# Attention and a gated product: issue order by fixed step gaps against issue order by a list scheduler

## The chip, the cores and the metric

The kernel runs on one core of one Trainium2 chip. Five engines work in it, each with its own queue of instructions that it takes strictly in order: TensorE (PE), VectorE (DVE), ScalarE (ACT), GpSimd (POOL), and SyncE (SP), which here only issues transfers between the chip's large memory and the on-chip one (SBUF). They meet through semaphores: an instruction waits until what it needs is there, and everything behind it on its queue waits with it. Matrix products leave PE into PSUM, a memory of eight banks, and DVE or ACT read them from there; POOL cannot.

The metric is the device time of one execution in microseconds. Less is better.

## The reference

```python
k_p = k.reshape(B, H, Sp, pool, D).mean(axis=3)       # B, H, S, D = 8, 8, 576, 64; pool = 8; Sp = 72
v_p = v.reshape(B, H, Sp, pool, D).mean(axis=3)
scores = scale * np.matmul(q, k_p.transpose(0, 1, 3, 2))
scores = scores - np.max(scores, axis=-1, keepdims=True)
attn = np.exp(scores)
attn = attn / (np.sum(attn, axis=-1, keepdims=True) + 1e-09)
attn_out = np.matmul(attn, v_p)

x = attn_out.transpose(0, 2, 1, 3).reshape(B * S, H * D)          # 4608 x 512
a, b = x @ w_a, x @ w_b                                # w_a, w_b: 512 x 1536
out = a * b @ w_out                                    # w_out: 1536 x 512
```

Keys and values are averaged over groups of eight positions, so each query attends to 72 keys. The result feeds a gated product: two inner products, their elementwise product, and an outer product. All is float32 outside. Inside, each number is kept as a high part, rounded for TensorE, and a low part (the number minus its high part), and a product is made of three matmuls: high by high, high by low, low by high. That is why so many instructions are casts and subtractions.

## The kernel before

**Tiling.** The 4608 rows (tokens) are cut into twelve halves of 384, and two halves make a pair. The first pair is computed in the plain way (`normal`), half by half; for the five others (`block`) a scheme with seven products in place of eight is used (Strassen's, in the form of Winograd): the right operands are sums and differences of parts of x (`prepare` makes them, T1 to T4), the left ones are sums and differences of parts of the weights (`block_sums` makes them, S1 to S4). Features are taken in steps of 256, so there are six items (steps) per pair and 30 seven-product items in all. The first pair has eight items: two of half 0, four of both halves, two of half 1. After each item, `outer` multiplies the gated features by w_out and DVE or ACT adds the result to the rows `y` (`taken_outer`), which go out after the pair's last item.

**Three streams.** Attention runs in 40 chunks of up to 128 queries (`chunk`): cast the queries, scores on PE, maximum, difference, exponential, sum, division, cast and split of the weights, transposes on PE, product with the values on PE. Keys and values of each of the eight batches are averaged by `load_keys` and `load_values`. Only three chunks belong to half 0, and the first weight product needs them. Meanwhile the weights, which arrive as 64-bit words, are converted (`convert_weights`: two ACT scalings and two DVE joins for each of 12 features and three matrices), split (`split_inner`, `split_outer`) and stored to memory (`keep`), since SBUF cannot hold them all. From then on every pass streams them back in (`load_parts`).

**What sets the order.** The program is written out by generators under the class `Chains` (lines 81 to 115). Its time is not in microseconds: it is a count of steps, and one step is about one group of matmuls on PE. A chain says "go on after so many steps", and the gaps are constants at the head (`PROBS_GAP`, `VALUE_GAP`, `CHUNK`, `KEYS_AHEAD`, `STORE_AFTER`, `BLOCK_STEPS` and so on). Which engine does a subtraction is written in the code. PE's main loop (lines 1038 to 1060) goes through the items in order, and between two groups of the present item it puts one group of `outer` of the item before:

```python
for _ in (normal if item[0] == "n" else block)(item):
    if next(before, "over") != "over":
        step()
```

**Tiles.** `Ring` gives out tiles in fixed rings: three of 4 KB per partition for raw weights, four and four for inner weight parts (`we`, `ws`), four for outer ones (`wo`): 15 in all, and each use has its own. The loads of the inner parts go round two or three rings in a fixed turn. In PSUM, attention has two banks (`att`), the inner products have four (`XA`, `XB`, `YA`, `YB`), the outer ones two (`acc`); the three chunks of half 0 also use the four (`early_bank`). The block sums are made, stored, and in every round, the first too, loaded from memory (`wanted`). Weight words are loaded by ACT's DMA queue, everything else by SP's.

## Time and profile before

| | |
|---|---|
| median of 3 runs | 1124.23 us (1123.45 to 1126.3) |
| profiled execution, its own time | 1121.22 us |
| profiled execution, span from first to last instruction | 1119.4 us |
| mean granted clock of PE | 0.966 |
| PE busy | 1013.6 us (91%), 5424 matmuls |
| DVE, ACT, POOL busy | 638.4, 466.7, 503.0 us |
| moved by DMA | 251.6 MB, 225 GB/s in the mean |

Shares of busy time are means over stages with different limits, so the prediction reads them by stretch. A busy PE is not a PE at its peak, since matmuls overlap and a lower granted clock makes each of them longer. In the list of groups a line is a line of the kernel; all subtractions for low parts have line 209, so there one goes by the names of the tiles. A row "A <- B" under waits says what A was waiting for last.

### The profile page before, as it was taken

The page shows a single profiled execution, that of the slowest core. Times are in us where ns is not written, and L with a number is a line of the kernel's source. Part 1 is how long each engine was busy: PE and PEld are TensorE (multiplying, and loading weights), DVE is VectorE, ACT ScalarE, POOL GpSimd, SP SyncE. Part 2 cuts the span into 40 slices and gives each one's busy share as a digit, 9 for nine tenths or more (in the row PEclk, how much of TensorE's full clock was granted, in tenths as well). Part 3 has the DMA queues.
Part 4 walks back from the last instruction along what each step waited for, and adds up shares of the span by engine and source line. Part 5 has one row for each costly group of instructions (what it writes and reads, how often), then busy time and mean ns, then how long its engine had stood idle before and what let it go on. Part 6 is the DMA issues. An engine that isn't in the chain of part 4 may idle for free.

```text
span 1119.4 us, 15231 instructions
## 1 busy us (share of the span) xinstructions
PE 1013.6 (91%) x5424; PEld 931.8 (83%) x5424; DVE 638.4 (57%) x1067; ACT 466.7 (42%) x1006; POOL 503.0 (45%) x462
## 2 busy tenths in 40 slices
PE   3368787998999979799999998999899999999998
PEld 3267687897889969789899897999799999999997
DVE  7697775746644653755754774463974453523333
ACT  3675656543445434334433444333434433322221
POOL 5344433374557855733333453433444442523322
PEclk9977799999989989899999999999999999999999
DMA  6687776458977985767644576456566455575441
GB/s 206 241 287 283 260 258 223 144 208 299 303 265 251 323 294 198 291 245 266 219 161 177 214 275 220 178 175 234 202 224 236 174 186 203 212 253 205 177 165 56
DMA packets 82586, 251.60 MB, mean 225 GB/s; under 512 B 12976, under 2 KB 12976, under 8 KB 82512
## 3 DMA queue, kind: packets, MB, share of 16 engines
q1 hardware_dynamic: 77328, 231.77, 58.5%
q10 hardware_dynamic: 5184, 18.88, 4.9%
q8 instruction: 43, 0.70, 0.2%
q14 instruction: 31, 0.25, 0.1%
HBM read 203.42 MB, written 47.19 MB: 224 GB/s over the span
## 4 chain that ended last, share of the span: by engine, by line
PE 59%; DVE 15%; DMA 13%; ACT 5%; POOL 3%; issue 3%; SPq 1%; ACTq 0%; POOLq 0%; DVEq 0%
PE acc_s L950 6%; PE acc_s L952 6%; PE acc_s L951 6%; DMA kept_S<-we 4%; PE psXA L868 3%; PE psXB L868 3%; PE psXA L870 3%; PE psXA L869 3%; PE psXB L869 3%; PE psXB L870 3%; DMA vraw<-in_vr 3%; DMA vraw<-in_v 2%; PE psYA L868 2%; PE psYB L868 2%; PE psYA L869 2%
## 5 line engine op out<-in xcount | busy, mean ns | idle before, releaser
L209 POOL TENSOR_TENSOR hh<-h,hh 128x384 fp32r<-128x384 f32 x144 | 150.6, 1052 | 128.6 <-ACT hh L905 80.8
L899 POOL TENSOR_TENSOR h<-h,h 128x384 f32<-128x384 f32 x90 | 98.1, 1090 | 231.5 <-DVE h L894 213.6
L975 DVE TENSOR_TENSOR y<-acc_s,y 128x512 f32<-128x512 f32 x150 | 102.9, 687 | 134.8 <-PE acc_s L952 134.5
L950 PE MATMUL acc_s<-wo,hh 128*128 128x512 f32 x360 | 144.8, 402 | 2.6 <-ACT y L973 2.6
L951 PE MATMUL acc_s<-wo,hh 128*128 128x512 f32 x360 | 142.8, 397 | 0.0
L952 PE MATMUL acc_s<-wo,hh 128*128 128x512 f32 x360 | 142.7, 396 | 0.0
L563 POOL TENSOR_TENSOR s<-s,z 128x576 f32<-128x576 f32 (+1 forms) x39 | 49.6, 1272 | 111.6 <-DVE z L561 102.3
L888 ACT COPY h<-psXA 128x384 f32<-128x384 f32 x90 | 43.1, 479 | 125.2 <-PE psXA L870 125.1
L952 PEld LDWEIGHTS acc_s<-wo,hh 128*128 128x128 f32 x360 | 68.2, 189 | 15.9
L950 PEld LDWEIGHTS acc_s<-wo,hh 128*128 128x128 f32 x360 | 68.3, 190 | 11.4 <-ACT y L973 2.9
L951 PEld LDWEIGHTS acc_s<-wo,hh 128*128 128x128 f32 x360 | 68.3, 190 | 8.3
L894 DVE TENSOR_TENSOR h<-psYA,h 128x384 f32<-128x384 f32 x60 | 33.2, 554 | 65.8 <-PE psYA L870 58.7
L905 ACT CAST hh<-h 128x384 fp32r<-128x384 f32 x90 | 45.5, 515 | 58.6 <-POOL h L899 58.2
L557 ACT ACTIVATE s<-s 128x576 f32<-128x576 f32 (+1 forms) x40 | 27.4, 685 | 100.9 <-DVE s L509 100.9
L598 PEld LDWEIGHTS ptr<-ident,pr 128*128 128x128 f32 (+1 forms) x320 | 36.1, 146 | 38.0 <-ACT pr L572 15.3
L599 ACT CAST turned<-ptr 128x512 fp32r<-128x512 f32 (+1 forms) x80 | 43.2, 544 | 55.8 <-PE ptr L598 53.7
L209 POOL TENSOR_TENSOR pr<-s,pr 128x512 fp32r<-128x512 f32 (+1 forms) x40 | 52.9, 1323 | 25.2 <-ACT pr L572 19.5
L598 PE MATMUL ptr<-ident,pr 128*128 128x128 f32 (+1 forms) x320 | 40.6, 253 | 25.8 <-ACT pr L572 12.2
L544 DVE TENSOR_REDUCE s<-psc 128x144 f32<-128x288 f32 (+1 forms) x104 | 42.7, 449 | 36.3 <-PE psc L541 36.2
L432 DVE TENSOR_REDUCE vp<-vraw 128x64 f32<-128x512 f32 (+1 forms) x42 | 27.4, 678 | 34.1 <-DMA vraw<-in_v 22.3
L209 DVE TENSOR_TENSOR ql<-tmp,qh 128x512 fp32r<-128x512 f32 (+1 forms) x37 | 34.5, 932 | 19.3 <-ACT qh L490 19.3
L572 ACT CAST pr<-s 128x512 fp32r<-128x512 f32 (+1 forms) x40 | 24.8, 621 | 49.1 <-POOL s L563 49.1
(359 smaller groups left out, 3053.2 us busy)
## 6 DMA issues: line engine op xcount, KB each, us to landing
wo<-kept_o SPq DMA_DIRECT2D x64, 512.0 KB, 4.7
we<-kept_S SPq DMA_DIRECT2D x44, 512.0 KB, 5.6
ws<-kept_S SPq DMA_DIRECT2D x44, 512.0 KB, 6.2
ws<-kept SPq DMA_DIRECT2D x41, 512.0 KB, 6.1
we<-kept SPq DMA_DIRECT2D x33, 512.0 KB, 4.7
raw<-kept_S SPq DMA_DIRECT2D x32, 512.0 KB, 3.8
kept<-we SPq DMA_DIRECT2D x24, 512.0 KB, 5.8
kept_S<-we SPq DMA_DIRECT2D x24, 512.0 KB, 6.0
```

What stands on the lines that cost most here:

```text
L209: eng.tensor_tensor(out=lo, in0=src, in1=hi.bitcast(F32), op=ALU.subtract)
L563: (nc.vector if first and i % 2 else nc.gpsimd).tensor_tensor(out=s[:n], in0=s[:n], in1=z[:n].unsqueeze(2).broadcast_to([n, H, SP]), op=AL ...
L598: nc.tensor.transpose(ptr[:rows, g, :n], src, ident[:n, :n])
L868: nc.tensor.matmul(pt, e[:, 0, m, c], xo[:, 0, kk], start=(opens and kk == 0), stop=False, **more)
L869: nc.tensor.matmul(pt, e[:, 0, m, c], xo[:, 1, kk], start=False, stop=False, **more)
L870: nc.tensor.matmul(pt, e[:, 1, m, c], xo[:, 0, kk], start=False, stop=(kk == 1), **more)
L899: nc.gpsimd.tensor_tensor(out=t, in0=t, in1=a, op=ALU.mult)
L905: nc.scalar.copy(e[:, 0], t)
L950: nc.tensor.matmul(pt, e[:, 0, cs], wos[y][:, 0], start=(y == 0), stop=False)
L951: nc.tensor.matmul(pt, e[:, 0, cs], wos[y][:, 1], start=False, stop=False)
L952: nc.tensor.matmul(pt, e[:, 1, cs], wos[y][:, 0], start=False, stop=(y == 1))
L975: nc.vector.tensor_tensor(out=acc[row], in0=pt, in1=acc[row], op=ALU.add)
```

## The change

`Chains` and `Ring` go. In their place stands `Machine`, a model of the five engines in microseconds, run while the program is built. Each piece of work asks for an engine (`on_pe`, `on_act`, `on_dve`, `either`, `transfer`) with a price and a rank; whenever the model's engine is free, it takes the waiting piece of the lowest rank and issues its instructions, and the piece goes on when the model says that it has ended, plus 0.25 us (`SETTLE`). So the order on each queue is the order in which the model's engine took the work.

- Ranks: attention chunks and weight features by a due time in microseconds, computed from fixed lengths of the items (27.0 for a block, 13.0 for a half); releases of tiles and readings of PSUM first (`TOP`), loads of parts 1e3, `outer` and stores 1e4, inner products 2e4. So PE takes attention first, then an outer group as soon as its operands are ready, and an inner group otherwise.
- `either`: subtractions, the gate's product and the division of the weights go to DVE or POOL, whichever the model has free first. Before, the engine was fixed.
- All transfers go through SP, the weight words too; the model lets SP run at most 3 us ahead of the landings, at 300 KB/us.
- `Slots`: one set of 15 tiles of 4 KB for early inputs, raw weights, words, inner and outer parts, raw reloads, sums and T2, each kind with a quota. Four smaller tiles (`tmp`) have quotas of their own.
- PSUM: until the first weight product all six banks besides `acc` serve attention; then it keeps two.
- Block sums of the first round are used straight from the tile in which they were made (they are stored as well); four inner parts that nobody reads again are no longer stored.
- The weights of attention lie in two fixed tiles with a 73rd column of 1e-9, so that the sum includes it; for batches 1 to 7 the keys are scaled over all four head pairs at once.

The number of matmuls is the same.

```diff
-class Chains:
-    def step(self, groups=1):
-        due = []
-        while self.chains and self.chains[0][0] <= self.now:
-            due.append(heapq.heappop(self.chains))
...
+    def take(self, engine):
+        queue = self.queues[engine]
+        while queue and queue[0][-1]["taken"]:
+            heapq.heappop(queue)
+        if not queue or self.free[engine] > self.now:
+            return False
+        asked = heapq.heappop(queue)[-1]
+        asked["taken"] = True
+        time = asked["time"][engine]
+        asked["issue"](engine)
+        end = self.free[engine] = self.now + time
+        self.later(end, None)
+        if engine == "SP":
+            self.landing = max(self.landing, end + 1.2) + asked["bytes"] / 300e3
+            self.free[engine] = max(end, self.landing - BACKLOG)
+            self.later(self.free[engine], None)
+            self.later(self.landing + 1.0, asked["job"])
+        else:
+            self.later(end if engine == "PE" else end + self.SETTLE, asked["job"])
+        return True
...
+def dve(n, ops=1):
+    return 0.1 * ops + 0.0012 * n
+def act(n, ops=1):
+    return 0.07 * ops + 0.00093 * n
+def pool(n, ops=1):
+    return 0.2 * ops + 0.00225 * n
+def mms(count, n):
+    return count * max(0.113, 0.013 + 0.00043 * n)
...
+QUOTA = {"early": 10, "raw": 3, "words": 3, "own": 4, "wo": 4, "load": 7, "raw2": 3, "sum": 4, "T2": 1}
+NSLOT = 15
...
+    def either(n, issue, ops=1):
+        return {"time": {"DVE": dve(n, ops), "POOL": pool(n, ops)}, "issue": lambda e: issue(engines[e])}
...
-        low_part(nc.gpsimd if first else nc.vector, ql[:, :, :n], qraw[:, :, :n], qh[:, :, :n])
+        yield low(NK * n, ql[:, :, :n], qraw[:, :, :n], qh[:, :, :n])
...
-            nc.scalar.dma_start(areas[f % 2], w_dram[name][:, f, :].bitcast(I32))
+            yield transfer(areas[f % 2], w_dram[name][:, f, :].bitcast(I32), 1 << 19)
...
-        nc.vector.tensor_reduce(out=z[:n], in_=s[:n], axis=AX.X, op=ALU.add)
-        nc.vector.tensor_scalar_add(z[:n], z[:n], 1e-9)
-        nc.vector.reciprocal(z[:n], z[:n])
+            nc.vector.tensor_reduce(out=z[:n], in_=wide[:n], axis=AX.X, op=ALU.add)
+            nc.vector.reciprocal(z[:n], z[:n])
...
+            if x in second and name[1] in ("S1", "S2", "S3", "S4"):
+                yield lambda: name in sums
+                loaded[x] = "sum", name, sums[name]
+                continue
+            yield lambda: name in kept and slots.can("load")() and x - taken["i"] < 9
...
+    psum = {"free": ["att0", "att1", "XA", "XB", "YA", "YB"], "att": {"att0", "att1"}, "opening": True}
...
+                    yield on_pe(mms(6, DM), products, 1e4)
+                yield on_pe(mms(6, HB), products, 2e4)
...
-        before = iter(())
-        for x, item in enumerate(items):
...
+        start(1e4, outer())
+        start(2e4, inner())
+        m.run()
```

More of the change, by code (lines that the diff above doesn't have):

```diff
@@ L87, in mark @@
+NSLOT = 15
+class Machine:
+    SETTLE = 0.25
+    def __init__(self):
+        self.now, self.count = 0.0, 0
+        self.queues = {e: [] for e in ("PE", "DVE", "ACT", "POOL", "SP")}
+        self.free = dict.fromkeys(self.queues, 0.0)
+        self.events, self.waiting, self.done = [], [], set()
+        self.landing = 0.0
     def mark(self, *what):
         self.done.add(what)
-    def wait(self, *marks):
-        while not all(m in self.done for m in marks if not isinstance(m[-1], int) or m[-1] >= 0):
-            yield 1
@@ L94, in start, with until @@
-    def start(self, chain, rank, after=0):
+    def until(self, *marks):
+        marks = [m for m in marks if not isinstance(m[-1], int) or m[-1] >= 0]
+        return lambda: all(m in self.done for m in marks)
+    def start(self, rank, task):
         self.count += 1
-        heapq.heappush(self.chains, (self.now + after, rank, self.count, chain))
-    def resume(self, chain, rank):
-        later = next(chain, None)
-        if later == self.PE:
-            self.count += 1
-            heapq.heappush(self.wanting, (rank, self.count, chain))
-        elif later is not None:
-            self.start(chain, rank, later)
@@ L325, in block_sums, with split_outer @@
+    def split_outer(f):
+        yield until(("weight", "o", f))
+        yield lambda: slots.can("wo")() and order_o[next_o[0]] == ("own", f)
+        next_o[0] += 1
+        e = slots.take("wo", ("own", f), [P, 2, 512], F32R)
+        w = rawt.pop(("o", f))
+        yield on_act(512, lambda: nc.scalar.copy(e[:, 0], w))
+        yield low(512, e[:, 1], w, e[:, 0])
+        tmps.give("o", f)
+        parts["o", f] = e
+        start(1e4 + f, keep("wo", ("o", f), e, False))
     def block_sums(j):
@@ L354, in block_sums, with load_raw @@
+            e = slots.take("sum", (j, name), e_shape, F32R)
+            yield on_act(512, lambda: nc.scalar.copy(e[:, 0], t))
+            yield low(512, e[:, 1], t, e[:, 0])
+            sums[j, name] = e
+            start(1e4, keep("sum", (j, name), e, False))
         for f in (2 * j, 2 * j + 1):
-            raws.give(("raw2", f))
+            slots.give("raw2", f)
         mark("sums", j)
+    def load_raw(f, t):
+        yield transfer(t.rearrange("p m c -> p (m c)"), kept["raw", f], 1 << 19)
+        mark("raw2", f)
@@ L620, in chunk @@
             if p > 1:
-                yield from wait(("prepared", p - 1))
+                yield until(("prepared", p - 1))
+            else:
+                yield lambda: all(("raw", f) in kept for f in range(3))
             if p not in xraw:
@@ new lines, in load_outer, with inner @@
+    def load_outer():
+        for x, name in enumerate(order_o):
+            if name[0] == "own":
+                continue
+            yield lambda: at_item[0] >= NJ - 1 and name in kept and slots.can("wo")() and next_o[0] == x
+            next_o[0] += 1
+            e = slots.take("wo", x, [P, 2, 512], F32R)
+            start(1e3 + x, load_one(x, ("wo", x, e), e.bitcast(F32).rearrange("p l c -> p (l c)"), kept[name], loaded_o))
+    def inner():
+        for number, item in enumerate(items):
+            at_item[0] = number
+            if item[0] == "n":
+                yield from normal(item)
+            else:
+                yield from block(item)
@@ new lines, in give_slot, with finish @@
+    def give_slot(e):
+        yield m.SETTLE
+        slots.give(e[0], e[1])
+    first_gate = {}
+    gated_in = [0]
+    def finish(item, f, half, h, key):
+        number = items.index(item)
+        need = sum(2 * len(x[1]) if x[0] == "n" else 4 for x in items[:number])
+        yield lambda: gated.can("hh")() and gated_in[0] >= need
+        gated_in[0] += 1
+        e = gated.take("hh", (item, f, half), [P, 2, HB], F32R)
+        yield on_act(HB, lambda: nc.scalar.copy(e[:, 0], h))
+        yield low(HB, e[:, 1], h, e[:, 0])
+        gates.give("h", key)
+        gs[item, f, half] = e
```

1333 lines of the change are left out of this document (680 added, 653 removed).

## The prediction

> **What bounds the kernel now.** I read the page's head and its slices first, then busy time by stretch, then what TensorE (PE) waited for, then the opening on VectorE (DVE), the groups of instructions and the DMA issues.
>
> ```profile
> span 1119.4 us, 15231 instructions
> PE 1013.6 (91%) x5424; PEld 931.8 (83%) x5424; DVE 638.4 (57%) x1067; ACT 466.7 (42%) x1006; POOL 503.0 (45%) x462
> PEclk9977799999989989899999999999999999999999
> ```
>
> PE is the bound of the whole, but not of every stage. The next view has, for each stretch: its length, then busy time and count of PE, PE's weight loads, DVE, ACT and POOL, then the granted clock, the DMA share and GB/s. The cuts are the first product with the weights (62.6), the first seven-product block (292.9), and places where the idle time changes.
>
> ```profile
> 0.00:62.60 62.60, 24.78 (x110) 20.97 (x111) 46.25 (x79) 30.25 (x64) 29.46 (x37) 0.99 0.65 216
> 62.60:292.90 230.30, 197.74 (x1049) 182.22 (x1049) 157.25 (x244) 126.19 (x262) 105.73 (x88) 0.90 0.70 249
> 292.90:480.00 187.10, 168.86 (x895) 154.57 (x894) 102.50 (x179) 78.16 (x172) 117.43 (x100) 0.95 0.78 278
> 480.00:820.00 340.00, 326.53 (x1791) 300.56 (x1792) 205.60 (x352) 137.16 (x307) 141.15 (x133) 0.99 0.61 213
> 820.00:980.00 160.00, 160.00 (x890) 148.68 (x889) 80.97 (x142) 63.20 (x138) 68.68 (x64) 1.00 0.57 202
> 980.00:1100.00 120.00, 120.00 (x624) 111.60 (x624) 37.93 (x62) 29.79 (x62) 35.81 (x36) 1.00 0.52 185
> 1100.00:1119.40 19.40, 15.66 (x74) 13.16 (x72) 7.90 (x12) 1.92 (x4) 4.78 (x5) 0.99 0.21 81
> 80.00:100.00 20.00, 15.68 (x61) 14.16 (x60) 18.82 (x26) 12.78 (x27) 11.07 (x9) 0.54 0.80 284
> ```
>
> An order can only win back idle PE time and the clock that idling costs; the change keeps all 5424 matmuls. Idle is length minus PE busy, lost clock is length times one minus clock:
>
> - start: 37.8 + 0.6 = 38.4
> - opening: 32.6 + 23.0 = 55.6
> - first round of blocks: 18.2 + 9.4 = 27.6
> - 480 to 820: 13.5 + 3.4 = 16.9
> - 820 to 1100: 0
> - tail: 3.7 + 0.2 = 3.9
>
> Together 142 us, so no order goes below some 977 us, and the last 280 us have nothing left to give. What PE waited for (total us, times, longest):
>
> ```profile
> PE ptr L598 <- ACT turned L599: 17.4, 11, 4.6
> PE ptr L598 <- ACT pr L572: 12.2, 6, 5.3
> PE psXA L868 <- DMA ws<-kept_S: 9.0, 2, 5.8
> PE psc L524 <- ACT kdiag L388: 8.9, 2, 8.1
> PE psc L524 <- DVE ql L209: 8.4, 5, 2.9
> ```
>
> These are few and long. The first is a transpose that waits until ScalarE (ACT) has emptied one of the two banks that attention shares. DVE in the opening, in order of time:
>
> ```profile
> 32.20 0.77 DVE L278 SCALAR_TENSOR_TENSOR words_a<-raw_first,words_a 128x512 int32<-128x512 int32 x1 [0.40 <-ACT words_a L275]
> 42.74 0.69 DVE L278 SCALAR_TENSOR_TENSOR words_o<-tmp,words_o 128x512 int32<-128x512 int32 x1 [3.13 <-ACT words_o L275]
> 46.36 1.76 DVE L282 SCALAR_TENSOR_TENSOR raw_first<-raw_first,words_b 128x512 int32<-128x512 int32 x1
> 48.04 1.40 DVE L375 TENSOR_REDUCE tmp<-kraw 128x72 f32<-128x576 f32 x2
> ```
>
> From 32.20 to 46.36 ten joins of weight words, at 0.68 us or more each, and then the key sums of the next batch stand on DVE ahead of the last early query chunk, without which no product starts.
>
> **The change, part by part.** The sum is made against the profiled execution: span 1119.4, its own time 1121.22, so 1.8 us lie around it; the median of the runs shown, 1124.23, is 3.0 above that.
>
> *Work removed.* The added 1e-9 becomes a constant column, the scaling of keys is done in half as many instructions, and 24 of 120 reloads of the block sums go:
>
> ```profile
> L560 DVE TENSOR_SCALAR z<-z 128x8 f32<-128x8 f32 x32 | 10.0, 314 | 1.1
> we<-kept_S SPq DMA_DIRECT2D x44, 512.0 KB, 5.6
> ws<-kept_S SPq DMA_DIRECT2D x44, 512.0 KB, 6.2
> raw<-kept_S SPq DMA_DIRECT2D x32, 512.0 KB, 3.8
> kept_S<-we SPq DMA_DIRECT2D x24, 512.0 KB, 6.0
> SPq L752 <- DMA kept_S<-we: 48.0, 9, 8.4
> words_a<-in_wa ACTq DMA_DIRECT2D x6, 512.0 KB, 4.9
> ```
>
> The 10 us of DVE lie under PE work (DVE is busy for 57%), so I price them at nothing; without that cover they are 0.31 us per chunk. In the first round the sums are used from the tile in which they were made, instead of going out (6.0 us) and back (6.2 us) first. That takes away PE's 9.0 us and, at that stretch's 9.4 of clock per 18.2 of idle, 4 us more: **13 us**. What is late next there is the sum itself, made of a POOL or DVE operation, an ACT cast and a second subtraction; it is released two blocks ahead, some 45 us. It goes to between 0 and 13. SyncE also stops waiting 48 us for those stores with the loads behind it.
>
> *Weight words moved from ACT's DMA queue to SP's.* 36 transfers (six groups of six like the last row) now queue behind SP's own. SP is planned to a 3 us backlog, the words rank ahead of all stores, and each is asked for as soon as its area has been read, one step ahead; DMA is 0.70 busy there. I take nothing; the bound is one late word (4.9 us) in the first feature block, inside the bounds of the opening.
>
> *Start (0 to 62.6).* Attention of the first half now ranks before the words on every engine, and all six free banks serve it. At least 6.8 us of joins and 1.4 us of key sums leave the way, and ACT's matching scalings with them: 10 us. Bounds: 0, if the joins are needed at once for the first product, and 20.
>
> *Opening (62.6 to 292.9).* Its 55.6 us are the bank and chunk waits above plus a cold clock (0.54 between 80 and 100, where DVE is busy 18.8 of 20 us and POOL only 11.1). The change lets either engine take a subtraction and fills PE with a product whenever a chunk is not ready. I take 38 of 55.6; bounds 10 (DVE stays full) and 55.6.
>
> *Rest of the middle.* Without the 9.0 and its clock, 27.6 + 16.9 - 13 = 31.5 us are left of hand-set gaps that came too short or too late. I take 25, bounds 0 and 31.5.
>
> *What it adds: hand-offs with no slack.* Before, an output product is spread over the next block, so its operands have 20 us to spare; now output and attention groups are put on PE's queue at the moment the plan has them ready. If they are late, PE stops, and every product behind waits, though its operands are there. The plan's prices against the rows:
>
> ```profile
> L894 DVE TENSOR_TENSOR h<-psYA,h 128x384 f32<-128x384 f32 x60 | 33.2, 554 | 65.8 <-PE psYA L870 58.7 <-POOL pr L209 4.0 <-POOL hh L209 3.0
> L899 POOL TENSOR_TENSOR h<-h,h 128x384 f32<-128x384 f32 x90 | 98.1, 1090 | 231.5 <-DVE h L894 213.6 <-PE po L640 17.8
> L209 POOL TENSOR_TENSOR hh<-h,hh 128x384 fp32r<-128x384 f32 x144 | 150.6, 1052 | 128.6 <-ACT hh L905 80.8 <-ACT hh L782 41.0 <-DMA kept_raw<-raw_first 3.6
> L905 ACT CAST hh<-h 128x384 fp32r<-128x384 f32 x90 | 45.5, 515 | 58.6 <-POOL h L899 58.2
> L572 ACT CAST pr<-s 128x512 fp32r<-128x512 f32 x32 | 19.9, 621 | 39.6 <-POOL s L563 39.6
> L574 ACT CAST rem<-s 128x64 fp32r<-128x64 f32 x64 | 12.4, 241 | 0.0
> L209 DVE TENSOR_TENSOR ql<-tmp,qh x37: 407/693/2314, 44.6 to 909.1; 128x512 fp32r<-128x512 f32 x29, 128x256 fp32r<-128x256 f32 x8
> ```
>
> DVE at 384 is planned at 0.56 us (0.554 measured), POOL at 1.06 (1.05 and 1.09): right. ACT is planned too fast: 0.43 against 0.515, and 0.81 for the three casts of a chunk against 0.621 + 2 x 0.241 = 1.10. So an operand is 0.1 to 0.3 us late from prices alone. The last row gives minimum, median and maximum of one DVE operation with two SBUF inputs: 0.69 normally, 2.31 at worst, as long as if it stood behind a POOL operation. The plan prices the two engines as if they never met. If DVE meets POOL 45% of the time (POOL's share) and waits half of 1.05, that is 0.24 per operation, 0.48 for two in a chain.
>
> Hand-offs: 40 chunks with four each (scores, two kinds of transposes, values), and 72 outputs (36 items, a half at a time): 232. Six matmuls take 6 x 120/624 = 1.15 us, and PE is somewhere inside such a group when an operand comes due, so lateness L costs L x L / 2.3: 0.02 us for 0.2, 0.10 for 0.48; and all 0.48 if nothing absorbs it. I take 0.10, since the price errors are at the low end and DVE, taking part of POOL's work at 0.55 instead of 1.05, shortens POOL's share. 232 x 0.10 = 23 us, and with clock lost as from 480 to 820 (3.4 per 13.5 idle, a quarter) **29 us**. Ends: 5 and 111.
>
> A rule of the Trainium skill bears on that last quarter: in "TensorE: Matmul & The Clock Gate" (What's actually happening) the clock falls only after an idle window of about 3.4 us. By it, waits of a fraction of a microsecond would cost no clock, and the sum would be 6 us lower. The 80:100 row shows 0.54 with PE busy 15.7 of 20 us, so on this trace the gate is not that lenient, and I keep the quarter.
>
> Sum: -10 (start) - 38 (opening) - 13 (sums kept) - 25 (middle) + 29 (hand-offs) = -57; span 1062, time 1064 against 1121.2, and 1067 at the level of the median.
>
> **Rivals.**
>
> *The opening stays.* For it: DVE's 18.8 of 20 us, and joins that can't leave DVE. Against it: POOL's 11.1. Start 0 and opening 10 give -10 - 13 - 25 + 29 = -19: 1105.
>
> *The hand-offs are free.* PE's queue and the plan's 0.25 us allowance after each operation absorb all: 5 in place of 29, 1043. The plan prices PE a little slow (six at 384 as 1.07, six at 512 as 1.40, so 14 and 6 groups 23.3 us, against 120 x 0.192 = 23.1), which speaks against it: PE runs ahead of its feeders.
>
> *Slower: VectorE and GpSimd stand in each other's way.* Every subtraction may go to either engine, so both run two-input operations side by side; one is held for the length of the other's, and DVE's strict order passes it on to the next chain. Place: the waits ahead of transposes, values and outputs. Price: 0.48 on all 232, 111 us, and half the opening's gain gone: -10 - 19 - 13 - 25 + 111 = +44, 1168. It turns the result from the point where waits reach (10 + 38 + 13 + 25) / (232 x 1.25) = 0.30 us on average. For it: 2.31 at most; against: the median 0.69. The Trainium skill's "SBUF — State Buffer" (SBUF: two separate sides) states it: the two engines' shared port pair is an exclusive lock held for a whole instruction. The trace's 2.31 us agrees.
>
> *The shared tiles run out.* Quotas add up to 39 tiles, there are 15; in later rounds 7 inner tiles are loaded ahead instead of up to 11. If PE waits 2 us per block for a load in the last 24, 48 us: 1115, no change to within 10 us. DMA at 0.52 to 0.61 there speaks against it.
>
> **How the numbers follow.** Forecast 0.42, opening stays 0.20, hand-offs free 0.15, slower 0.18, tiles run out 0.05. The forecast's own range is 1045 to 1090; with the rivals on the fast side (full opening: 1025) and up to the edge of slower, 1020 to 1132. Changes under 0.3% (3.4 us) can't be told from none: faster 0.75, within 0.06, slower 0.19.
>
> **What would show it.** First weight product before 55; first block before 262, with a clock above 0.95 in between; no wait on kept_S in the first round; PE's waits many and under 0.5 us. Between 820 and 1100 the old kernel had none: idle time there measures the hand-offs alone. Wrong if DVE's two-input operations grow well past 0.7 us and PE's waits name them, or if PE waits for loads.

## The result, and the profile after

The changed kernel takes 1061.72 us (median of 4 runs, 1060.16 to 1062.2); beside it on the same chip the kernel before takes 1123.84 (4 runs, 1122.45 to 1126.3). The ratio is 0.9443, 95% interval 0.9423 to 0.9462: faster by 5.6%, some 62 us. The forecast was 1067. The profiled execution has a span of 1059.5 us where the sum gave 1062.

The page's head and its line of granted clock, kernel after:

```profile
span 1059.5 us, 15170 instructions
PE 994.5 (94%) x5424; PEld 913.7 (86%) x5424; DVE 764.8 (72%) x1204; ACT 464.5 (44%) x992; POOL 336.7 (32%) x273
PEclk9997899999999999999999999999899999999999
```

DVE is busy 126 us longer than before (638.4), though it has only 137 instructions more, and POOL has 189 fewer. Those two numbers turn out to be the main thing to explain. Busy time by stretch, kernel after; the columns are length, PE, weight loads, DVE, ACT, POOL, granted clock, DMA share, GB/s. The cuts answer to those of the prediction: first weight product at 47.9, first seven-product block at 253.2, then the places where idle time changes. The last row is a window inside the second:

```profile
0.00:47.90 47.90, 24.47 (x117) 21.49 (x117) 41.70 (x70) 31.36 (x68) 27.61 (x37) 1.00 0.85 293
47.90:253.20 205.30, 187.00 (x1040) 172.50 (x1041) 168.69 (x245) 119.16 (x245) 91.58 (x67) 0.95 0.73 255
253.20:440.00 186.80, 179.19 (x991) 162.78 (x990) 164.25 (x251) 89.39 (x194) 89.73 (x64) 0.99 0.71 246
440.00:760.00 320.00, 309.92 (x1704) 285.52 (x1703) 226.66 (x370) 129.33 (x283) 80.10 (x64) 0.99 0.58 207
760.00:1040.00 280.00, 278.87 (x1508) 258.85 (x1507) 154.93 (x258) 92.88 (x200) 45.61 (x40) 1.00 0.58 202
1040.00:1059.50 19.50, 15.10 (x72) 12.51 (x70) 8.54 (x14) 2.39 (x5) 2.02 (x2) 0.95 0.21 81
80.00:100.00 20.00, 9.58 (x44) 7.67 (x44) 19.57 (x29) 7.92 (x19) 11.72 (x10) 0.79 0.65 226
```

With the prediction's reckoning (idle plus lost clock) the excess is now:

| stretch | before | after | forecast of the change | measured |
|---|---|---|---|---|
| start, to the first weight product | 38.4 | 23.4 | -10 | -15.0 |
| opening, to the first block | 55.6 | 18.3 + 10.3 = 28.6 | -38 | -27.0 |
| from there until 820 before, 760 after | 27.6 + 16.9 = 44.5 | 9.5 + 13.3 = 22.8 | -13 - 25, and part of +29 | -21.7 |
| the last rounds | 0 | 1.1 | the rest of +29 | +1.1 |
| tail | 3.9 | 5.4 | 0 | +1.5 |
| sum | 142 | 81 | -57 | -61 |

So the total came out within 3 us of the span, but not by each term being right: the opening gave 11 us less than forecast, the start 5 more, and the hand-offs, priced at 29, are not where they were priced. What PE waited for, kernel after (total us, times, longest):

```profile
PE ptr L799 <- DVE weights L681: 11.8, 4, 6.0
PE psc L718 <- ACT kdiag L504: 10.4, 2, 8.0
PE psXB L1082 <- DVE h L1115: 5.8, 4, 3.3
PE ptr L799 <- ACT pr L771: 4.3, 2, 2.7
PE psXA L1082 <- ACT h L1109: 3.1, 2, 1.7
```

The forecast was "many and under 0.5 us". Added up, the whole view has 45 waits, 60.6 us (before: 61 waits, 102.0 us). Seventeen of the 45 are under 0.5 us, and together they make 5 us; the other 28 make up nearly all the time. Fifteen, 23.4 us, lie ahead of the first weight product. So waits are few and long, not many and short. No row names kept_S. PE's timeline shows where they are (start, duration, instruction, and in brackets the wait before it and what ended it); kernel after:

```profile
83.28 0.66 PE L799 MATMUL ptr<-ident,pr 64*128 64x64 f32 x4 [4.65 <-DVE weights L681]
...
99.53 0.72 PE L799 MATMUL ptr<-ident,pr 128*128 128x128 f32 x4 [5.96 <-DVE weights L681]
...
425.32 0.50 PE L1157 MATMUL acc_s<-wo,hh 128*128 128x512 f32 x1 [2.09 <-DVE y L1186]
...
583.09 0.44 PE L1082 MATMUL psXA<-xB,load 128*128 128x384 f32 x1 [1.74 <-ACT h L1109]
...
747.54 0.69 PE L1082 MATMUL psXB<-xB,load 128*128 128x384 f32 x1 [3.33 <-DVE h L1115]
```

The first two rows lie in the opening, the others at changes from one pair to the next. From 253 to 1040, the waits of half a microsecond or more stand at 279 (0.91 us) and round 410 to 425, 576 to 586, 737 to 748 and at 908. Those last four places are the four changes of pairs. Elsewhere PE hardly waits. At a pair change `prepare` runs for the next pair (sums over 768 columns, casts, subtractions) while the blocks still need their products read from PSUM. The change at 745 on DVE and then on POOL, kernel after (start, duration):

```profile
740.12 0.51 DVE L1121 TENSOR_TENSOR h<-psYA,h 128x384 f32<-128x384 f32 x1
740.54 2.29 DVE L759 TENSOR_TENSOR weights<-weights,z 128x576 f32<-128x576 f32 x1
742.75 2.19 DVE L242 TENSOR_TENSOR hh<-h,hh 128x384 fp32r<-128x384 f32 x1
...
746.95 0.54 DVE L1115 TENSOR_TENSOR h<-psXB,h 128x384 f32<-128x384 f32 x1
```
```profile
740.35 1.86 POOL L242 TENSOR_TENSOR xT<-xraw,xT 128x768 fp32r<-128x768 f32 x1
742.16 2.37 POOL L242 TENSOR_TENSOR xB<-xraw,xB 128x768 fp32r<-128x768 f32 x1
744.67 1.94 POOL L242 TENSOR_TENSOR xT<-xraw,xT 128x768 fp32r<-128x768 f32 x1
```

DVE's division of 128x576 ends 0.6 us after POOL's first subtraction, and its subtraction of 128x384, 0.55 us in the ordinary case, takes 2.19 and ends 0.4 us after POOL's second. The read of psXB that PE waits 3.33 us for (line 1115) stands behind both in DVE's strict order. The read of PSUM at 740.12, which POOL's subtraction overlaps, keeps its 0.51 us. POOL's second subtraction began while the division held DVE, and it takes 2.37 us where the first took 1.86. This is the slower rival's mechanism, at work; what it costs is the question of the experiments.

### The profile page after: what moved, and what is told of

Read it like the earlier page. It is cut to its first block, busy times and chain, and to the rows that moved or that the text cites. A ratio compares the mean times of both kernels' runs of the same rounds, so it can differ in the third digit from the quotient of the medians.

```text
span 1059.5 us, 15170 instructions
## 1 busy us (share of the span) xinstructions
PE 994.5 (94%) x5424; PEld 913.7 (86%) x5424; DVE 764.8 (72%) x1204; ACT 464.5 (44%) x992; POOL 336.7 (32%) x273
## 4 chain that ended last, share of the span: by engine, by line
PE 78%; DVE 15%; issue 2%; DMA 2%; POOL 1%; ACT 1%; SPq 0%; POOLq 0%; DVEq 0%; ACTq 0%
PE acc_s L1157 8%; PE acc_s L1159 8%; PE acc_s L1158 8%; PE psXB L1082 4%; PE psXA L1082 4%; PE psXB L1084 4%; PE psXB L1083 4%; PE psXA L1083 3%; PE psXA L1084 3%; PE psYA L1082 3%; PE psYB L1082 3%; PE psYB L1083 3%; PE psYA L1083 3%; PE psYA L1084 3%; PE psYB L1084 3%; PE ptr L799 2%
## 5 line engine op out<-in xcount | busy, mean ns | idle before, releaser
L242 POOL TENSOR_TENSOR hh<-h,hh 128x384 fp32r<-128x384 f32 x56 | 61.2, 1094 | 233.4 <-ACT hh L1038 199.0
L1038 ACT CAST hh<-h 128x384 fp32r<-128x384 f32 x144 | 73.8, 514 | 103.9 <-DVE h L1127 42.1
L242 DVE TENSOR_TENSOR hh<-h,hh 128x384 fp32r<-128x384 f32 x88 | 65.5, 747 | 31.7 <-ACT hh L1038 30.6
L759 POOL TENSOR_TENSOR weights<-weights,z 128x576 f32<-128x576 f32 (+1 forms) x29 | 36.3, 1252 | 161.5 <-DVE z L754 127.6
L750 ACT ACTIVATE weights<-weights 128x576 f32<-128x576 f32 (+1 forms) x40 | 27.5, 687 | 90.4 <-DVE weights L681 90.1
L1127 POOL TENSOR_TENSOR h<-h,h 128x384 f32<-128x384 f32 x23 | 27.8, 1208 | 103.4 <-DVE h L1121 103.3
L696 DVE TENSOR_REDUCE weights<-psc 128x144 f32<-128x288 f32 (+1 forms) x104 | 43.6, 447 | 19.0 <-PE psc L740 18.7
L799 PE MATMUL ptr<-ident,pr 128*128 128x128 f32 (+1 forms) x320 | 36.6, 257 | 19.9 <-DVE weights L681 11.8
L1082 PE MATMUL psXA<-xT,load 128*128 128x384 f32 x156 | 53.5, 343 | 0.9 <-DVE h L1121 0.9
L1082 PE MATMUL psXB<-xT,load 128*128 128x384 f32 x156 | 53.1, 341 | 0.0
L1084 PE MATMUL psXA<-xT,load 128*128 128x384 f32 x156 | 52.4, 336 | 0.0
L1084 PE MATMUL psXB<-xT,load 128*128 128x384 f32 x156 | 52.4, 336 | 0.0
```

What stands on the lines that cost most here:

```text
L242: eng.tensor_tensor(out=lo, in0=src, in1=hi.bitcast(F32), op=ALU.subtract)
L696: nc.vector.tensor_reduce(out=s[:n, 2 * g:2 * g + 2, :], in_=pt[:n, :2 * hk].rearrange("p (w h s) -> p h s w", w=2, h=2), axis=AX.X, op=AL ...
L799: nc.tensor.transpose(ptr[:rows, g, :n], src, ident[:n, :n])
L1038: yield on_act(HB, lambda: nc.scalar.copy(e[:, 0], h))
L1082: nc.tensor.matmul(pt, w[:, 0, mat, c], xo[:, 0, kk], start=(opens and kk == 0), stop=False, **more)
L1084: nc.tensor.matmul(pt, w[:, 1, mat, c], xo[:, 0, kk], start=False, stop=(kk == 1), **more)
```

## The experiments

All are edits of the kernel after, unless said otherwise; each was timed in three rounds against the kernel before, whose medians lay between 1123.11 and 1124.68 in these groups. Differences are taken to the change's 1061.72; since the kernel before itself moves by 1.6 us between groups, a difference of 2 or 3 us isn't told apart.

**1. Sums of the first round reloaded.** The term of 13 us by itself.

```diff
-            start(1e4, keep("sum", (j, name), e, False))
+            start(1e4, keep("sum", (j, name), e, True))
...
-    second = range(4 * LEAD, 4 * LEAD + 7 * NJ)
+    second = range(0)
```

> The changed kernel, but the block sums of the first round are loaded back from memory, as in the kernel before. Theory (the prediction's term): the round trip is worth 13 us, so 1075 (1071 to 1079), with PE waits on loads of kept_S between 250 and 410. Rival: the plan finds cover for the 24 loads, and the 9 us of the old kernel came from its fixed turn of rings and not from the round trip: within 3 us of 1061.7, no PE wait on kept_S.

1075.6 us (1073.75 to 1078.11), ratio 0.9575 [0.9533, 0.9618]: 13.9 us more. PE's waits for the sums themselves, on its timeline in this kernel, and the stretch of the first round (PE 172.60 in the kernel after, at clock 0.99):

```profile
266.00 0.44 PE L1082 MATMUL psXA<-xT,load 128*128 128x384 f32 x1 [0.88 <-DMA load<-kept_S]
271.36 0.44 PE L1082 MATMUL psYA<-xT,load 128*128 128x384 f32 x1 [2.98 <-DMA load<-kept_S]
```
```profile
260.00:440.00 180.00, 163.21 (x881) 148.20 (x881) 133.48 (x216) 81.26 (x176) 89.75 (x67) 0.97 0.82 295
```

The size is confirmed, its inside only in part: the two waits on kept_S make 3.9 us, not 9. The rest is lost in the same 180 us through other waits (PE busy 163.2, and the clock 0.97) with DMA at 0.82 instead of 0.71 of its time. That the busier DMA made attention late is a reading of these rows; no run separates it.

**2. Two banks for attention from the start.** This takes away more than the change had added: in the kernel before, only the transposes were held to two banks, while scores and value products of the first three chunks also used the other four.

```diff
-    psum = {"free": ["att0", "att1", "XA", "XB", "YA", "YB"], "att": {"att0", "att1"}, "opening": True}
+    psum = {"free": ["att0", "att1"], "att": {"att0", "att1"}, "opening": False}
```

> The changed kernel, but attention has two PSUM banks from the start instead of six until the first weight product. Theory (banks are a good part of the opening's gain): the first weight product comes 5 us or more later than 47.9 and the time rises by 5 to 15 us, PE waits on ACT's reading of transposes. Rival (DVE bounds the start, with 41.7 us busy of 47.9): under 3 us, because DVE's work is the same and PE waits for it either way.

1062.88 us (1061.9 to 1063.38), ratio 0.9462 [0.9416, 0.9509]: no difference. Inner products of the first pair and of the blocks (minimum, median, maximum ns, then first and last start), two banks:

```profile
L1009 PE MATMUL psXA<-xB,own x40: 334/342/615, 59.7 to 214.7; 128*128 128x384 f32 x40
...
L1082 PE MATMUL psXA<-xB,load x60: 334/337/446, 254.3 to 1024.4; 128*128 128x384 f32 x60
```

The first weight product comes at 59.7 instead of 47.9, and yet the first block is at 254.3 instead of 253.2. Between 80 and 100 this kernel has PE busy 18.09 of 20 us at a clock of 0.98, where the kernel after has 9.58 and 0.79: it starts late and then runs without the waits of 4.65 and 5.96. So start and opening are one stage with one end, and what an earlier start wins there is waited for again. The forecast had added the two as if they were independent.

**3. Words of the first two features before attention**, on SP, ACT and DVE, much as they stood before the change.

```diff
-            start(due_f[f] + delay - 6, load_words(f))
+            start(due_f[f] + delay - 106, load_words(f))
         for f in range(NF):
-            rank = due_f[f] + delay
+            rank = due_f[f] + delay - (100.0 if f < 2 else 0.0)
```

> The changed kernel, but the weight words of the first two features rank ahead of attention, on SP, ACT and DVE, much as they stood in the kernel before. Theory (the prediction's term for the start): the first weight product comes 10 us later and the time rises by about 10. Rival (as with the two banks, a later start is made up by 100, since DVE has the same work to do before half 1 is ready): under 3 us.

1084.29 us (1083.58 to 1084.56), ratio 0.9636 [0.9618, 0.9654]: 22.6 us more, over twice the 10 of the term. The same two kinds of row, this kernel:

```profile
L1009 PE MATMUL psXA<-xB,own x40: 334/338/686, 56.6 to 235.8; 128*128 128x384 f32 x40
...
L1082 PE MATMUL psXA<-xB,load x60: 334/337/522, 275.5 to 1046.3; 128*128 128x384 f32 x60
```

The first weight product is 8.7 us late, the first block 22.3, and the rest follows unchanged. Against experiment 2 this is the telling pair: a start that is 11.8 us late through banks costs nothing, one that is 8.7 us late through the order on DVE and ACT costs 22.6. The order counts, not the moment of the first product.

**4. Half of the joins left out.** Of the two DVE operations that put a weight word together the second isn't issued, while the plan still prices both; the order is that of the change. The weights are then not fully converted, so this kernel computes less.

```diff
-                nc.vector.scalar_tensor_tensor(
-                    out=wi, in0=wi, scalar=-(1 << 31), in1=low_bits, op0=ALU.bitwise_and, op1=ALU.bitwise_or
-                )
```

> The changed kernel with its plan untouched, but the second of the two joins of each weight word is not issued (the weights then have wrong bits): 36 DVE operations of 0.8 us, some 29 us, go from the first 220 us. Theory (DVE bounds the opening): the first seven-product block, at 253.2, comes 10 to 20 us earlier and the waits of 4.65 and 5.96 us between 80 and 100 shrink by more than half. Rival (the opening is bound by the latency of the chains, not by DVE's work): under 4 us.

1048.95 us (1048.3 to 1051.86), ratio 0.9328 [0.9306, 0.935]: 12.8 us less. The page's busy line and the first block (lines are three lower here):

```profile
PE 990.5 (95%) x5424; PEld 912.1 (87%) x5424; DVE 731.3 (70%) x1168; ACT 463.3 (44%) x992; POOL 330.3 (32%) x273
```
```profile
L1079 PE MATMUL psXA<-xB,load x60: 334/337/446, 241.8 to 1010.7; 128*128 128x384 f32 x60
```

DVE's busy time falls by 33.5 us and the first block comes 11.4 us earlier, nearly the whole gain. In the kernel after, DVE is busy 41.70 + 168.69 = 210.4 of the first 253.2 us. So DVE's work is one of the things that hold the opening, at about a third of a microsecond for each microsecond of it removed; it isn't the only one. Of the two long waits that were to shrink by more than half, that of 4.65 us falls to 1.96, that of 5.96 only to 5.55.

**5. No allowance.** The plan's 0.25 us after each operation is what was to keep hand-offs from being late.

```diff
-    SETTLE = 0.25
+    SETTLE = 0.0
```

> The changed kernel, but the plan reckons with no time between the end of an operation and the start of the next engine (0 in place of 0.25 us), so it believes operands ready 0.5 to 1.0 us too early. Theory (the prediction's formula, lateness L costs L*L/2.3 at each of 232 hand-offs): L of 0.75 gives 0.24 each, 57 us, with the clock 70: 1115 to 1135. Rival (hand-offs are absorbed, since the changed kernel shows no idle PE at all in the middle of its rounds): under 6 us, and the stretches without idle time stay so.

1093.6 us (1092.7 to 1095.26), ratio 0.9736 [0.9695, 0.9777]: 32 us more, half of the gain gone. Two of PE's waits at the second of those pair changes, on this kernel's timeline:

```profile
604.19 0.44 PE L1082 MATMUL psXA<-xT,load 128*128 128x384 f32 x1 [3.37 <-DVE h L1121]
606.70 0.69 PE L1082 MATMUL psXB<-xT,load 128*128 128x384 f32 x1 [0.90 <-DVE h L1121]
```

The whole view of PE's waits has 66, together 79.2 us, against 45 and 60.6; the mean clock is 0.973 against 0.985 (1.2% of 1093 is 13 us). 18.6 + 13 is about the 32. So hand-offs that are late do cost, as the prediction held, but about half of what its formula made of this edit, and again most of the long waits are at pair changes and in the opening (first block at 267.0; one of 3.22 us stands at 323), not spread over 232 places. Neither theory's number was met: the allowance is worth something between the two.

**6. Outputs later.** The products with w_out of an item wait until PE has begun the next item: slack for the 72 hand-offs of outputs.

```diff
-        for item in items:
+        for number, item in enumerate(items):
...
-                yield lambda: all((item, 2 * j + y, half) in gs for y in range(2))
+                yield lambda: all((item, 2 * j + y, half) in gs for y in range(2)) and at_item[0] > min(number, len(items) - 2)
```

> The changed kernel, but an output product may start only when PE has begun the next item, as in the kernel before, so its operands have most of an item to spare. Theory (hand-offs cost something): the 72 output hand-offs go, 72 x 0.10 x 1.25 = 9 us, 1053. Rival (they cost nothing, the trace has 2.1 us of waits on them in all): within 4 us, or slower, because the tiles between the products are held longer and PE finds less to do at the change of pairs.

1068.98 us (1068.06 to 1069.15), ratio 0.9513 [0.9474, 0.9552]: 7.3 us more. Slack for the outputs wins nothing. PE's waits in the two kernels are alike until 735; after that this one has more at the last two pair changes; that fewer output groups are left to fill in there is a reading. In the kernel after, PE's waits for the outputs' operands (`hh`) come to 2.0 us in all, so the 72 outputs' share of the 29 us was small.

**7. Every free choice goes to DVE.** `either` offers DVE alone: the rival of VectorE and GpSimd by itself.

```diff
-        return {"time": {"DVE": dve(n, ops), "POOL": pool(n, ops)}, "issue": lambda e: issue(engines[e])}
+        return {"time": {"DVE": dve(n, ops)}, "issue": lambda e: issue(engines[e])}
```

> The changed kernel, but every operation that may go to either engine is planned on DVE alone; POOL keeps only what it does in the first microseconds. No DVE operation can then stand behind a POOL operation. Theory (the two engines stand in each other's way): DVE's two-input operations at 384 fall to 0.56 us without exception, and since POOL's 337 us come back as some 180 us on DVE (945 of 1060), the time stays within 15 of 1061.7; PE's waits at the change of pairs get shorter. Rival (what matters is that there are two engines): DVE is full in the opening already (19.6 of 20 us), so the opening grows by 20 us or more and the time to over 1085.

1045.12 us (1044.18 to 1045.51), ratio 0.9288 [0.927, 0.9305]: 16.6 us less than the change. The page's head, this kernel:

```profile
span 1043.7 us, 14942 instructions
PE 992.7 (95%) x5424; PEld 917.4 (88%) x5424; DVE 798.1 (76%) x1456; ACT 470.4 (45%) x992; POOL 8.9 (1%) x21
```

POOL gives up 328 us of work, and DVE, which takes over all of it, 252 instructions, is busy only 33 us longer; the expectation had 945 us. One and the same operation on DVE (minimum, median, maximum ns), first two rows from the kernel after, then two from this one:

```profile
L242 DVE TENSOR_TENSOR hh<-h,hh x88: 517/558/2391, 56.6 to 1047.5; 128x384 fp32r<-128x384 f32 x88
...
L1127 DVE TENSOR_TENSOR h<-h,h x67: 536/559/2101, 259.6 to 1044.7; 128x384 f32<-128x384 f32 x67
```
```profile
L242 DVE TENSOR_TENSOR hh<-h,hh x144: 506/552/560, 50.3 to 1031.9; 128x384 fp32r<-128x384 f32 x144
...
L1127 DVE TENSOR_TENSOR h<-h,h x90: 500/552/559, 267.1 to 1029.5; 128x384 f32<-128x384 f32 x90
```

The medians are the same; without POOL beside it no operation is longer than 0.56 us, with it the longest is 2.39. The groups' means tell the sum, kernel after and then this one:

```profile
L242 DVE TENSOR_TENSOR hh<-h,hh 128x384 fp32r<-128x384 f32 x88 | 65.5, 747 | 31.7 <-ACT hh L1038 30.6
L1127 DVE TENSOR_TENSOR h<-h,h 128x384 f32<-128x384 f32 x67 | 49.7, 741 | 2.1
```
```profile
L242 DVE TENSOR_TENSOR hh<-h,hh 128x384 fp32r<-128x384 f32 x144 | 79.0, 552 | 22.0 <-ACT hh L1038 20.5
L1127 DVE TENSOR_TENSOR h<-h,h 128x384 f32<-128x384 f32 x90 | 49.5, 550 | 0.7
```

0.19 us in the mean on each. An estimate for all of DVE takes each group of the kernel after at this kernel's mean: at these prices its operations would be some 98 us shorter. Operations with an input in PSUM and reductions add nothing to that. The 252 further operations cost some 160 us, so the durations should grow by 62 us, and they do grow by 58 (808 to 866). The page's busy time grows by less, 33 us, because it counts a stretch in which two operations overlap once. So about 98 us of DVE's time went with POOL's presence. This agrees with the Trainium skill, "SBUF — State Buffer" (SBUF: two separate sides), whose shared port pair is locked for a whole instruction; here 0.56 becomes up to 2.39. What that was worth on PE's side is seen from 440 to 760, where the kernel after has 309.92:

```profile
440.00:760.00 320.00, 319.67 (x1792) 296.76 (x1791) 255.83 (x475) 140.76 (x306) 0.00 (x0) 1.00 0.62 220
```

The waits at the pair changes of 580 and 745 are gone; the first block comes later (258.2 against 253.2), the rest after it is 785.5 us long instead of 806.3. Three things differ at once in this run: DVE never stands behind POOL, POOL's slower operations leave the chains, and the plan's prices for DVE now hold. No run tells them apart. The rows at 740 show the first at work; against a large share of the second, PE's waits that name POOL come to only 0.6 us after the first block of the kernel after, though a chain can also carry the delay on through another engine.

**8. The gates' operations fixed on POOL**, with the free choice left for everything else: does the choice itself matter, or what it is used for?

```diff
-        yield low(HB, e[:, 1], h, e[:, 0])
+        yield fixed(HB, lambda eng: low_part(eng, e[:, 1], h, e[:, 0]))
...
-                yield either(HB, lambda eng: eng.tensor_tensor(out=t, in0=t, in1=a, op=ALU.mult))
+                yield fixed(HB, lambda eng: eng.tensor_tensor(out=t, in0=t, in1=a, op=ALU.mult))
```

> The changed kernel, but the gates' product and the gates' low part go to POOL alone, as in the kernel before; everything else stays free. Theory (the free choice is a large part of the gain because it takes this work off POOL's 1.05 us and chains get shorter): 8 us or more slower, 1070 to 1085. Rival (the chains have room, outputs begin mostly in the next item anyway): within 4 us, with DVE's busy time falling by some 70 us and POOL's rising by some 150.

1059.06 us (1057.65 to 1059.68), ratio 0.9415 [0.9394, 0.9436]: 2.7 us less than the change, with overlapping intervals, so not told apart. DVE has 686.8 us and POOL 457.1. Moving the gates back to where they were before neither loses nor clearly wins: choosing an engine for them freely was no part of the gain. POOL works 120 us more here and the time is no longer, and the wait of 3.33 us at the third pair change is 0.52. So it isn't the amount of POOL's work that costs, but which of it stands where.

**9. The kernel before with POOL's work on DVE.** If POOL is a hindrance, is DVE alone also better in the old order? All fifteen places that name GpSimd for an operation (the memsets apart) are rewritten like this one; base: the kernel before.

```diff
-            nc.gpsimd.tensor_tensor(out=t, in0=a, in1=b, op=op)
+            nc.vector.tensor_tensor(out=t, in0=a, in1=b, op=op)
```

> The kernel before, with its own order, but every operation of POOL (except the clearing of tiles) on DVE. It tells the order apart from the choice of engines. Theory 1 (the order made the gain, and the old order leaves chains room): DVE takes over 503 us of POOL's work at about half its price, loses its waits behind POOL, and ends near 800 us busy; the time stays within 15 of 1124. Theory 2 (POOL was what held the old kernel back, the scheduler gained by using it less): 1085 to 1105, a third to two thirds of the change's gain without any scheduler. Third (the old fixed gaps fit the old engines only): DVE's queue comes late to PSUM, over 1140.

1131.91 us (1127.72 to 1135.41), ratio 1.0067 [1.0041, 1.0093]: 0.7% slower. Its busy line:

```profile
PE 1014.1 (90%) x5424; PEld 930.1 (83%) x5424; DVE 800.3 (71%) x1519; ACT 468.1 (42%) x1006; POOL 4.5 (0%) x10
```

DVE's load is that of experiment 7, 798.1, and the time is 87 us longer. So in the old order the choice of engines alone gains nothing; the gain is made by the order, together with what came with it (the pooled tiles, the banks, and the reloads saved, 13.9 us by experiment 1). Giving up POOL paid under the new order and not under the old one, whose hand-set gaps were left as they were; gaps set anew for DVE alone are an untested rival.

**10. POOL in the opening only**: `either` offers both engines until the last item before the blocks, and DVE alone after that.

```diff
-        return {"time": {"DVE": dve(n, ops), "POOL": pool(n, ops)}, "issue": lambda e: issue(engines[e])}
+        return {"time": {"DVE": dve(n, ops), "POOL": pool(n, ops)} if at_item[0] < first_s - 1 else {"DVE": dve(n, ops)}, "issue": lambda e: issue(engines[e])}
```

> The changed kernel; the free choice holds until the last item ahead of the seven-product blocks, afterwards DVE alone. Theory (POOL helps where DVE is full and hurts elsewhere): the first block starts at 253 as in the changed kernel, 5 us ahead of the run with DVE alone, and the rest is as there: 1040. Rival (POOL's lock costs as much in the opening as it gives): 1045 within 3.

1043.91 us (1042.42 to 1047.14), ratio 0.9302 [0.9278, 0.9325]. Against experiment 7 it is 1.2 us less, with overlapping intervals (by the ratio it is even the slower one): no difference told, though its first block stands at 251.5, 6.7 us ahead of 258.2. The 1040 expected wasn't reached. It does show that the loss through POOL comes nearly all after the opening, since taking POOL away there alone gives 17.8 us.

**11. DVE alone, and ACT's prices as measured.** The plan had ACT too fast (0.43 us for the 0.515 of a 384-column cast).

```diff
-    return 0.07 * ops + 0.00093 * n
+    return 0.12 * ops + 0.00098 * n
```

> DVE alone, and the plan's price of ACT raised to what the trace shows (0.12 us per operation and 0.98 ns per element, so 0.50 for 384 and 1.24 for the two scalings of a word, in place of 0.43 and 1.09). All PE waits over 1 us left in the run with DVE alone but one lie in the first 112 us, the longest (9.1) on an ACT cast. Theory (the plan believes ACT ahead of where it is, and puts PE's transposes too early): that wait shrinks below 4 us, first block at 250, 1038. Rival (DVE's work bounds the opening, the order only shifts the wait): 1045 within 3.

1042.48 us (1041.32 to 1043.35), ratio 0.9279 [0.9264, 0.9294]: 2.6 us less than experiment 7, with overlapping intervals, so not told apart. The longest wait, for attention's casts in the first 112 us, falls from 9.1 to 7.5 us, where the theory had it below 4, and the first block is at 256.3, not 250. So the rival holds: the price errors that stood at the head of the hand-off sum are worth some 3 us at most once DVE works alone.

**12. In addition, three items of half 0 first, not two** (`LEAD`): the opening then starts with more products that need only the first three chunks, and the rest of attention and of the weights gets more time.

```diff
-LEAD = 2
+LEAD = 3
```

> DVE alone and ACT's prices as in the run before; besides, three items in place of two use half 0 alone before half 1 is needed (LEAD 3), and three come after for half 1 alone. The matmuls are the same. Theory (PE's waits of 2.0 and 7.5 us between 80 and 105 stand there because half 1 is due while DVE still converts weights; 13 us more of products that need half 0 alone cover them): those waits shrink below 2 us, first block at 248, 1034 to 1038. Rival (the third item needs features 4 and 5 earlier, so DVE has the same work before the same point): within 3 us of 1042.5, the waits in other places.

1035.02 us (1033.35 to 1036.72), ratio 0.9206 [0.9174, 0.9238]: 7.5 us less than experiment 11, 26.7 less than the change, and 88.9 less than the kernel before in the same group. It is the fastest of all. The page's head, and the first block (256.3 in experiment 11):

```profile
span 1034.9 us, 14979 instructions
PE 988.0 (95%) x5424; PEld 913.3 (88%) x5424; DVE 797.3 (77%) x1456; ACT 471.5 (46%) x992; POOL 8.8 (1%) x21
```
```profile
L1082 PE MATMUL psXA<-xB,load x60: 334/337/442, 247.9 to 999.1; 128*128 128x384 f32 x60
```

The first block is 8.4 us earlier, as expected: the gain lies in the opening, the place where the forecast had hoped for 38 and got 27. The waits there don't all shrink below 2 us: that of 7.5 is gone, but one of 2.0 stays at 82 and one of 3.6 stands at 103, now for the weights. Three items first with the free choice of engines wasn't tried, so how far experiments 7 and 12 add up by themselves is open.

## Why the prediction was right, and where it was not

**Bound and excess.** That an order can win only PE's idle time and the clock that it costs, and that the last rounds had nothing left to give, held: the excess fell by 61 us and the span by 60.

**Start (-10) and opening (-38).** Together 48 forecast and 42 by the excess; the first block is 39.7 us earlier. The single terms missed in opposite ways (15.0 and 27.0), because they are one stage: experiment 2 moves the first product by 11.8 us for nothing. The mechanism named for the start, attention ahead of the words, was right and is the larger part: undone, it costs 22.6 (experiment 3). The other one, six banks, was worth nothing. The first row of the old list, 17.4 us of waits for a bank, couldn't carry it. Ahead of the first weight product, the only stretch with six banks, stand two of them, kernel before:

```profile
35.08 0.42 PE L598 MATMUL ptr<-ident,rem 128*96 128x128 f32 x2 [2.13 <-ACT turned L599]
47.73 0.72 PE L598 MATMUL ptr<-ident,pr 128*128 128x128 f32 x4 [1.30 <-ACT turned L599]
```

The other 14 us come later, where the changed kernel has two banks too, and yet it waits there only 2.4 us for that copy. The step that failed there is "I take 38 of 55.6": the row with DVE busy 18.8 of 20 us between 80 and 100 was quoted as a bound, and it is 19.57 now. Experiments 4 and 12 confirm that the opening gives way when DVE has less to do or more time to do it.

**Sums kept (-13).** 13.9 when undone. Of its inside, 9.0 of waiting and 4 of clock (4.6 by its own rate), only 3.9 are waits on the reloads in the new order.

**Hand-offs (+29).** The mis-sized step, and in the wrong place. The formula spread 0.10 us over 232 hand-offs; measured is 1.1 us of excess from 760 to 1040, where the prediction said that hand-offs would show alone, and nothing to be won by slack for the outputs (experiment 6). PE's idle time from 253.2 to 1040 is 7.6 + 10.1 + 1.1 = 18.8 us. Of these, 9.8 us are waits of block products (line 1082) until a PSUM bank has been read, and the formula didn't count these as hand-offs at all. The other 9.0 us, over the 168 hand-offs or so that fall in this time (27 chunks, 60 outputs), are 0.05 each, half of the 0.10 taken; a few long waits make them up and nearly all hand-offs cost nothing. The allowance of 0.25 us, which the prediction put only with the rival of free hand-offs, is about the size of the price errors of 0.1 to 0.3 us: without it 32 us are lost (experiment 5). Nearly all that is left of idle time there sits at the pair changes, and the forecast knew no such place. By bookkeeping, -13 - 25 + 29 = -9 stood for what measured -20.6, and this made up for the 11 us that the opening fell short. That the total is so close is luck to that extent.

**The clock.** Three windows at pair changes, kernel after:

```profile
420.00:440.00 20.00, 17.27 (x85) 14.79 (x86) 16.81 (x31) 6.56 (x14) 5.32 (x4) 0.91 0.47 165
580.00:600.00 20.00, 17.15 (x87) 14.92 (x86) 16.46 (x25) 5.99 (x12) 7.64 (x6) 1.00 0.38 133
740.00:760.00 20.00, 16.67 (x75) 14.53 (x75) 17.06 (x25) 8.49 (x19) 9.53 (x8) 0.83 0.18 61
```

Waits of 0.68 to 2.09 us between 410 and 425 went with a granted clock of 0.91 from 420 to 440, and from 580 to 600, with waits of 1.74 and 1.11, it stayed 1.00; 3.33 us at 747 went with 0.83 from 740 to 760. Neither the quarter kept for short waits nor the rule of "TensorE: Matmul & The Clock Gate" (What's actually happening) in the Trainium skill, about 3.4 us, gives all three. The prediction's reason for not going by that rule stands: in the kernel before, the longest wait between 63 and 100 us is 2.1 us, and the clock from 80 to 100 was 0.54. Over the whole stretch from 253.2 to 1040 the quarter roughly fits (5.1 us of clock for 18.8 idle). For waits of a fraction of a microsecond, on which the 6 us hung, no run here has enough of them to say.

**The rivals.** Hand-offs free (1043) described the middle of the rounds rightly, and with DVE alone the total is there too (1045.12), though by another way. Tiles running out didn't happen: no wait of PE's list names a load of the blocks. VectorE against GpSimd was right as a mechanism, and the prediction's reading of its row (median 0.69, maximum 2.31) was right in both: operations grow to 2.39, the median stays. It was weighed against the median, though, while the mean is what counts: 0.19 us more on each of the commonest operations, some 98 us of DVE's time by the estimate of experiment 7, most of it hidden. Its price in time is at most about the 16.6 us of that run, not the 101 that separated 1168 from the forecast, for 0.05 us per hand-off is far below the 0.30 at which it would have turned the sign. That DVE takes work off POOL at 0.55 us instead of 1.05, quoted as a reason for a low price, was half of the truth: taking all of POOL's work cost DVE only 33 us more busy time than sharing it.

## What to carry to other kernels

A plan made with measured prices and a small allowance can hand work over with no slack and lose almost nothing in steady rounds; look for what is left where the kinds of work change, and price the stages that share an end as one. Before letting a scheduler choose between VectorE and GpSimd, compare the mean of a two-input operation with its median: where the mean is well above, as here, look whether the long ones lie beside work of the other engine, for then giving the work to one of the two may cost that engine little. Test an engine choice under the order it will run in, since the same choice lost 0.7% in the old order and won 1.6% in the new one.

## What the runs showed of the hardware that was not expected

All of GpSimd's 328 us of elementwise work fits onto VectorE for 33 us of added busy time (58 us of added durations), since VectorE's own operations get some 98 us shorter without GpSimd beside them. GpSimd seems to suffer as well: its subtractions of 768 columns (xB in the kernel after) take from 1.83 to 2.57 us, and the one at 742 that takes 2.37 began while VectorE's division was under way. What doesn't suffer is an operation of VectorE with one of its inputs in PSUM; one such group, kernel after (minimum, median, maximum ns):

```profile
L1121 DVE TENSOR_TENSOR h<-psYA,h x60: 497/556/560, 258.0 to 1043.2; 128x384 f32<-128x384 f32 x60
```

Sixty of them, none over 0.56 us, beside 67 of the same size with both inputs in SBUF (line 1127) that went up to 2.10. So in this kernel it is the operations with two inputs in SBUF that stood behind GpSimd. The section of the Trainium skill's "SBUF — State Buffer" named above (SBUF: two separate sides) limits the lock to these and to VectorE's two-port modes, and these rows agree with it.
